# The last feed-forward group in seven products instead of eight, interleaved with the group before it

## The chip, the cores and the metric

The kernel runs on one core of a Trainium2 chip. The metric is device time in microseconds (us) of one execution, the median of several. In the profile, PE is TensorE (matmuls), PEld its weight loads, DVE is VectorE, ACT is ScalarE, POOL is GpSimd and SP is SyncE, which issues most DMAs.

## The reference

Two stages. The first is a retention layer (attention without softmax, with a decay per head) over 8 batches, 8 heads, 576 positions and 64 values per head; the second is a two-layer feed-forward block on the 4608 rows that come out of it.

```
scores = scale * np.matmul(q, k.transpose(0, 1, 3, 2))
Dmat = np.where(rel >= 0, gamma[:, None, None] ** rel[None, :, :], 0.0)
attn = np.matmul(scores * Dmat[None, :, :, :], v)
x = attn.transpose(0, 2, 1, 3).reshape(B * S, H * D)      # 4608 x 512
h = x @ w_in                                              # 512 x 2048
out = (np.maximum(h, 0.0) ** 2) @ w_out                   # 2048 x 512, fp32
```

## The kernel before

**Units and groups.** The 4608 rows are cut into 36 units of 128 rows: four full chunks of a batch, and a "tail" unit that holds the last 64 rows of two batches. Two units make a group, so there are 18 groups, numbered 0 to 17. Per group the retention stage (scores, state sums, outputs; line L337 in the profile) leaves a transposed activation `xT` of 512 x 256. The feed-forward stage (`add_ff`) then makes 16 "FF1 blocks" of four matmuls with 256 columns each (L819). Two blocks share a PSUM bank; ACT takes it out with a relu (L827), and a square follows, on ACT (L837) or on DVE (L839). The squares fill `gT`, the 2048 x 256 input of the second layer. In this text "block 2.1 of group 4" is the second block of the third pair.

**The second layer in seven products.** Groups 0, 1 and 17 multiply `gT` with `w_out` directly, 16 matmuls of 512 columns for each unit (L860; the very last unit by halves of its columns, with a copy and a store for each half). Groups 2 to 16 go through `add_strassen`: the two units, the two halves of the 2048 inner values and the two halves of the 512 output columns make a 2 x 2 x 2 block product, which takes seven products of 8 matmuls with 256 columns instead of eight (L912). Differences of `w_out` (`wT`, L772) are made once. Four sums of the group's `gT` (`gS`, L890) are made by DVE for each group, each in two halves: S3 = A11 - A21, S1 = A21 + A22, S2 = S1 - A11, S4 = A12 - S2. Product P7 reads S3, P6 reads S2, P5 reads S1 and P3 reads S4. Bank "a" gathers P1, P6, P5 and P3 one on top of the other, and after each of the first three ACT copies what stands there (`p1`, `u2`, `u4`, L925). Bank "b" has P2 and bank "c" P7 and then P4. DVE adds banks and copies into the output tile: d11 = b + p1, d22 = c + u4 (this must be done before P4 adds to bank c), d21 = c + u2 (L935); ACT copies the fourth quarter (L955). SP stores each unit with one DMA (L792, L796).

**The order.** No order is written out by hand. Every piece of work is a task with an engine, a key, an assumed duration, its dependencies and the buffers that it takes and frees. `Schedule.emit` plays all of them through, on each engine always the ready task with the lowest key, and the instructions are issued in the order that comes out; after that each engine runs its own list strictly in order. An assumed duration or latency that is changed can therefore move the order of every engine. A DMA's results count as there 2.1 us after its issue slot. Keys of the feed-forward stage count in the units' time, 32 for a unit: FF1 block n of a group has the key `base + 2 n`, the products follow with `base2 + 0, 4, 8 ...`. Forty "warm" matmuls on a scratch tile (L241) have the highest key and fill PE in the front, where weights and inputs arrive (`FIRST` is the order of these loads; the weights are cast by ACT and POOL in halves, L316).

**Around the change.** The units of the last group are reversed, so that its first unit is the tail and its second a full one; its key base is that of the tail unit, after the whole of group 16. Its stores are issued by ACT's queue (L788). From group 11 to 16 the retention of one group is "joined" with the next group's scores; up to group 10 it is not, and then the outputs (`ret/fb`, L337) wait for the state sums, which DVE makes between the sums gS and the addition d22.

Of the kernel before, what the change touches and what calls it, by code (L numbers as in the profile page):

```python
# [9 lines left out]
FP32 = mybir.dt.float32  # L10
FP16 = mybir.dt.float16
ACTF = mybir.ActivationFunctionType
ALU = mybir.AluOpType
# [88 lines left out]
def kernel(  # L102
# [9 lines left out]
    nc = tc.nc  # L112
# [3 lines left out]
    P = 128  # L116
# [31 lines left out]
    g_pool = ctx.enter_context(tc.tile_pool(name="g", bufs=3))  # L148
    u_pool = ctx.enter_context(tc.tile_pool(name="u", bufs=1))
    r_pool = ctx.enter_context(tc.tile_pool(name="r", bufs=3))  # L150
# [64 lines left out]
    for hp in range(NP):  # L215
# [8 lines left out]
    EARLY = 20  # L224
    SQ_ACT = (0, 1, 2, 3, 4, 5, 6)
    JOIN = 11
    PAIRED = 8
    FIRST = ["k0", "q0", "v0", "k2", "q2", "w0", "v2", "w1", "w2", "w3", "w4", "w5", "w6", "w7", "k4", "q4", "v4", "k6", "q6", "v6"]
    sched = Schedule(dict(ff=4, prS=1, prO=1, g=3, ld=5, wst=4, kq=7, v16=7, rT=4, x=3, rl=3, o=4, p1=1, u2=1, u4=1,
                          R=6, Rm=6, kqT=6))  # L230
# [31 lines left out]
    def dma_task(key, dur, fn, **kw):  # L262
        t = add("SP", key, dur, fn, deps=list(last_load), **kw)
        last_load[:] = [t]
        return t
# [18 lines left out]
    def add_load_pair(name, u):  # L284
        b, c = units[u][1:]
        n = "kqv".index(name)

        def fn():
            if name != "q":
                tile_of["stage", u] = stage.tile([P, 2, H, 2 * D], FP32, name="pair", tag="wst")  # L290
            x = tile_of[name + "32", u] = tile_of["stage", u][:, n % 2]
            nc.sync.dma_start(out=x, in_=(k, q, v)[n][b, :, c * P:(c + 2) * P, :].rearrange("h (p e) d -> p h (e d)", e=2))
        loaded[name, u] = loaded[name, u + 1] = dma_task(0, 1.81 if loaded else 2.9, fn, acq=("wst",) if name != "q" else ())

    def add_weight(i):
        fb = i % 4

        def fn():
# [6 lines left out]
            tile_of["w", i] = t  # L305
        t = dma_task(0, 2.75, fn, acq=("wst",))
        dst = w_in16[:, :, fb * 512:(fb + 1) * 512] if i < 4 else w_out16[:, fb * 4:(fb + 1) * 4, :]
# [477 lines left out]

    def store(u, o, lo=0, hi=DM):
        kind, b, c = units[u]

        eng = nc.scalar if group_of[u] == len(groups) - 1 else nc.sync
        if kind == "full":  # L790
            r0 = b * S + c * P
            eng.dma_start(out=out[r0:r0 + P, lo:hi], in_=o[:, lo:hi])  # L792
        else:
            for i in range(2):
                r0 = (b + i) * S + 512
                eng.dma_start(out=out[r0:r0 + 64, lo:hi], in_=o[i * 64:(i + 1) * 64, lo:hi])  # L796
# [8 lines left out]
    def add_ff(g):  # L805
        us = groups[g]
        n = len(us)
        base = us[0] * L
        nf = 4 // n
        f1 = []  # L810
        sq = []
        for fb in range(NF // nf):
            for j in range(nf):
                def f(fb=fb, j=j):
                    if j == 0:
                        tile_of["ph", g, fb] = ps_ff.tile([P, nf, n * P], FP32, name="ph", tag="ff")
                    fi = nf * fb + j
                    for m in range(NP):
                        nc.tensor.matmul(tile_of["ph", g, fb][:, j, :], lhsT=w_in16[:, m, fi * P:(fi + 1) * P],  # L819
                                         rhs=tile_of["x", g][:, m, :], start=(m == 0), stop=(m == NP - 1))  # L820
                f1.append(add("PE", base + (nf * fb + j) * n, 0.01 + 0.2133 * n, f,
                              deps=[T["x", u] for u in us] + wcast_of(nf * fb + j) + f1[-1:],
                              acq=("ff",) if j == 0 else ()))
# [4 lines left out]

            on_act = n == 2 and g >= STRASSEN and fb in SQ_ACT

            def fg(fb=fb, on_act=on_act):
# [6 lines left out]
                else:  # L838
                    nc.vector.tensor_tensor(out=t, in0=rl, in1=rl, op=ALU.mult)  # L839
            r = add("ACT", base + 4 * fb + 4, 0.6, fr, deps=[f1[-1]], acq=("rl",))  # L840
            sched.free("ff", [r])
            sq.append(add("ACT" if on_act else "DVE", base + 4 * fb + 6, 0.63 if on_act else 0.45, fg, deps=[r] + sq[:1],
                          acq=() if fb else ("g",)))
            sched.free("rl", [sq[-1]])
        sched.free("x", [f1[-1]])
        base2 = base + NF * n
        if STRASSEN <= g < len(groups) - 1:
            add_strassen(g, us, base2, sq)
            return
        for s, u in enumerate(us):  # L850
            end = base2 + NF * (s + 1)
            f2 = T["ff2"][-1:] if s == 0 else f2[-1:]

            cuts = [(0, DM)] if u != groups[-1][-1] else [(0, HM), (HM, DM)]
            for ci, (lo, hi) in enumerate(cuts):
                for fi in range(NF):
                    def f(fi=fi, s=s, u=u, lo=lo, hi=hi):
                        if fi == 0:
                            tile_of["po", u, lo] = ps_ff.tile([P, hi - lo], FP32, name="po", tag="ff")
                        nc.tensor.matmul(tile_of["po", u, lo], lhsT=tile_of["g", g][:, fi, s * P:(s + 1) * P],  # L860
                                         rhs=w_out16[:, fi, lo:hi], start=(fi == 0), stop=(fi == NF - 1))
                    f2.append(add("PE", base2 + NF * s + fi / len(cuts) + 8 * ci, 0.0025 + 0.2135 / len(cuts), f,
                                  deps=[sq[fi // nf]] + wcast[4 + fi // 4] + f2[-1:],
                                  acq=("ff",) if fi == 0 else ()))

                def fo(u=u, lo=lo, hi=hi):
                    if lo == 0:
                        tile_of["o", u] = o_pool.tile([P, DM], FP32, name="o", tag="o")
                    nc.scalar.copy(out=tile_of["o", u][:, lo:hi], in_=tile_of["po", u, lo])
                oc = add("ACT", end + 1, 0.12 + 0.47 / len(cuts), fo, deps=[f2[-1]], acq=() if lo else ("o",))  # L870
                sched.free("ff", [oc])
                st = add(*(("ACT", end + 1.1, 0.05) if g == len(groups) - 1 else ("SP", -0.5, 0.7)),
                         lambda u=u, lo=lo, hi=hi: store(u, tile_of["o", u], lo, hi), deps=[oc], after=2.5)
            sched.free("o", [st])
        sched.free("g", [f2[-1]])
        T["ff2"].append(f2[-1])

    def add_strassen(g, us, base, sq):
        uA, uB = us
        G = lambda s, i, h: tile_of["g", g][:, i * HF + h * HF // 2:i * HF + (h + 1) * HF // 2, s * P:(s + 1) * P]  # L880
# [18 lines left out]
        s3[0]["acq"] = ("wst",)  # L899
        s1 = add_sum(0, base, lambda h: G(1, 0, h), lambda h: G(1, 1, h), ALU.add, lambda h: low(h) + high(h) + s3[:1])  # L900
        s2 = add_sum(1, base + 1, lambda h: Sx(0, h), lambda h: G(0, 0, h), ALU.subtract, lambda h: [s1[h]])
        s4 = add_sum(3, base + 4, lambda h: G(0, 1, h), lambda h: Sx(1, h), ALU.subtract, lambda h: [s2[h]])
        last = T["ff2"][-1:]
# [34 lines left out]

        p1 = product(1, 0, "a", raw(0, 0), wB[0, 0], low, True, True, [])
        c1 = on_act_copy("p1", "a", 5, [p1])  # L940
        p7 = product(7, 4, "c", summed(2), wT[2], lambda h: [s3[h]], True, True, [])
        p6 = product(6, 8, "a", summed(1), wT[1], lambda h: [s2[h]], False, True, [c1])
        c2 = on_act_copy("u2", "a", 13, [p6])
        p2 = product(2, 12, "b", raw(0, 1), wB[1, 0], high, True, True, [])
        d11 = on_dve_add(uA, 0, "b", "p1", 17, [p2, c1], ("o",))
        sched.free("ff", [d11])
        sched.free("p1", [d11])
        p5 = product(5, 16, "a", summed(0), wT[0], lambda h: [s1[h]], False, True, [c2])
        c4 = on_act_copy("u4", "a", 21, [p5])
        d22 = on_dve_add(uB, 1, "c", "u4", 22, [p7, c4], ("o",))  # L950
        sched.free("u4", [d22])
        p3 = product(3, 20, "a", summed(3), wB[1, 1], lambda h: [s4[h]], False, True, [c4])

        def f12():
            nc.scalar.copy(out=o_tile(uA)[:, HM:], in_=bank("a"))  # L955
        c12 = add("ACT", base + 25, 0.37, f12, deps=[p3, d11])
        sched.free("ff", [c12])
        p4 = product(4, 24, "c", raw(1, 1), wT[3], high, False, True, [d22])
        d21 = on_dve_add(uB, 0, "c", "u2", 29, [p4, d22])
        sched.free("ff", [d21])  # L960
        sched.free("u2", [d21])
        sched.free("wst", [p3])
        sched.free("g", [p4])
        T["ff2"].append(p4)
        for u, ds in ((uA, [d11, c12]), (uB, [d22, d21])):
            st = add("SP", -0.5, 0.7, lambda u=u: store(u, o_tile(u)), deps=ds, after=2.5)
            sched.free("o", [st])

# [43 lines left out]
```

## Time and profile before

| | |
|---|---|
| median of 4 runs | 298.94 us (298.76 to 299.13) |
| the profiled execution | 299.05 us, of which the span, first to last instruction, is 297.2 |
| PE | busy 286.0 us, 96% of the span, 4320 matmuls |
| DVE, ACT, POOL | busy 199.0, 187.4 and 93.3 us |
| granted TensorE clock | 0.998 of full speed |
| FF1 (L819) | 1152 matmuls |
| seven-product second layer (L912) | 840 matmuls |
| direct second layer (L860) | 112 matmuls |
| squares on ACT (L837) and on DVE (L839) | 112 at 630 ns, 32 at 554 ns |
| sums gS (L890) | 120, at 516 to 591 ns |

A line of the page gives a source line, an engine, an operation, its output and inputs with their shapes, a count, the busy time in us, the mean of one in ns, and the idle time of the engine just before it with what ended that idle time. The busy time of a matmul is longer than its share of PE, since matmuls overlap: what one costs is read from the distance of their starts.

### The profile page before, as it was taken

To read this page: it belongs to the slowest core of one execution; us is meant where nothing else is said; L and a number is where in the kernel's file an instruction comes from. 1 tells how busy PE (TensorE), PEld (TensorE's weight loads), DVE (VectorE), ACT (ScalarE), POOL (GpSimd) and SP (SyncE) were. 2 spreads that over 40 slices of the span, in tenths; PEclk is the share of its full clock that TensorE was granted. 3 is DMA by queue.
4 is the path that set the end of the run, shared out by engine and by line. 5 is a ranking of instruction groups with operands and counts; after the bars stand their busy time and mean duration, and the time that the engine had idled before them with its cause. 6 is when DMAs were issued, how large, how long until landed. Compare 5 with 4: busy or idle time off the path is not lost.

```text
span 297.2 us, 10048 instructions
## 1 busy us (share of the span) xinstructions
PE 286.0 (96%) x4320; PEld 233.4 (79%) x4320; DVE 199.0 (67%) x413; ACT 187.4 (63%) x354; POOL 93.3 (31%) x129
## 2 busy tenths in 40 slices
PE   8979999999989999999999999999999999999995
PEld 3558755688878888888788888788888888988874
DVE  4778469879495949593959597767777766462410
ACT  5247753484867676648576667756666666658861
POOL 4454384434232506152415142424241520000000
PEclk9999999999999999999999999999999999999999
DMA  7999999899999989999969699999999980101012
GB/s 204 326 372 386 360 263 228 213 193 175 210 144 216 195 190 169 209 185 211 178 157 165 151 186 214 213 161 211 156 213 156 218 146 18 73 3 71 2 71 73
DMA packets 139261, 54.14 MB, mean 182 GB/s; under 512 B 118096, under 2 KB 130640, under 8 KB 139216
## 3 DMA queue, kind: packets, MB, share of 16 engines
q1 hardware_dynamic: 138768, 52.97, 85.3%
q8 instruction: 34, 0.56, 0.8%
q10 hardware_dynamic: 448, 0.52, 0.6%
q14 instruction: 11, 0.09, 0.1%
HBM read 36.70 MB, written 9.44 MB: 155 GB/s over the span
## 4 chain that ended last, share of the span: by engine, by line
PE 63%; DVE 12%; ACT 10%; DMA 9%; issue 3%; POOL 2%; POOLq 0%
PE po L912 26%; PE ph L819 25%; DVE gS L890 6%; ACT rl L827 5%; ACT gT L837 4%; PE psO L337 4%; PE po L860 4%; DMA pair<-in_v_dram 3%; DMA wo<-in_moe_w_out_dram 3%; DMA pair<-in_k_dram 3%; PE warm L241 2%; DVE gT L839 2%; PE psc L337 1%; PE psS L337 1%; PE psT L412 1%
## 5 line engine op out<-in xcount | busy, mean ns | idle before, releaser
L819 PE MATMUL ph<-xT,w_in 128*128 128x256 f16 x1152 | 139.4, 273 | 0.0
L819 PEld LDWEIGHTS <-w_in 128*128 128x128 f16 x1152 | 111.2, 98 | 14.9 <-POOL w_in L316 0.3
L827 ACT ACTIVATE rl<-ph 128x512 f16<-128x512 f32 x144 | 84.1, 588 | 51.7 <-PE ph L819 49.1
L837 ACT ACTIVATE gT<-rl 128x512 f16<-128x512 f16 x112 | 70.6, 630 | 3.5
L890 DVE TENSOR_TENSOR gS<-gT 128x512 f16<-128x512 f16 x60 | 33.6, 560 | 39.1 <-ACT gT L837 38.5
L912 PEld LDWEIGHTS <-gS 128*128 128x128 f16 x480 | 45.6, 98 | 10.0 <-DVE gS L890 4.5
L912 PE MATMUL po<-wT,gS 128*128 128x256 f16 x360 | 49.2, 273 | 2.4 <-DVE gS L890 2.3
L361 POOL TENSOR_TENSOR v<-v,vdec_full 128x512 f16<-128x512 f32 x24 | 25.7, 1072 | 57.2 <-DMA v<-in_v_dram 48.2
L912 PEld LDWEIGHTS <-gT 128*128 128x128 f16 x360 | 34.8, 98 | 4.4 <-issue 0.2
L912 PE MATMUL po<-w_out,gT 128*128 128x256 f16 x240 | 31.1, 273 | 0.0
L349 POOL CAST kq<-k 128x512 f16<-128x512 f32 x28 | 18.8, 672 | 35.1 <-DMA k<-in_k_dram 34.7
L349 POOL CAST kq<-q 128x512 f16<-128x512 f32 x28 | 18.4, 656 | 27.1 <-DMA q<-in_q_dram 27.0
L839 DVE TENSOR_TENSOR gT<-rl 128x512 f16<-128x512 f16 x32 | 17.6, 554 | 13.6 <-ACT rl L827 13.2
L860 PE MATMUL po<-w_out,gT 128*128 128x512 f16 (+1 forms) x112 | 22.6, 349 | 0.1
L925 ACT COPY u<-po 128x256 f32<-128x256 f32 x30 | 11.0, 367 | 15.7 <-PE po L912 15.4
L698 DVE TENSOR_TENSOR xT<-psO,gam_full 128x512 f16<-128x512 f32 x28 | 18.4, 685 | 2.9 <-PE psO L337 2.6
L935 DVE TENSOR_TENSOR o<-po,u 128x256 f32<-128x256 f32 x30 | 12.6, 418 | 10.5 <-PE po L912 7.2
L637 DVE TENSOR_TENSOR rT<-psc,mask 128x512 f16<-128x512 f32 x28 | 18.5, 680 | 1.1 <-PE psc L337 1.1
L890 DVE TENSOR_TENSOR gS<-gS,gT 128x512 f16<-128x512 f16 x30 | 17.7, 591 | 1.0
L860 PEld LDWEIGHTS <-gT 128*128 128x128 f16 x112 | 10.6, 98 | 7.9 <-issue 0.3
L890 DVE TENSOR_TENSOR gS<-gT,gS 128x512 f16<-128x512 f16 x30 | 15.4, 516 | 1.0
L912 PE MATMUL po<-wT,gT 128*128 128x256 f16 x120 | 15.8, 273 | 0.2 <-DVE o L935 0.2
(78 smaller groups left out, 263.5 us busy)
## 6 DMA issues: line engine op xcount, KB each, us to landing
out_dram<-o SPq DMA_DIRECT2D x31, 256.0 KB, 2.7
k<-in_k_dram SPq DMA_DIRECT2D x24, 256.0 KB, 4.7
q<-in_q_dram SPq DMA_DIRECT2D x24, 256.0 KB, 5.2
v<-in_v_dram SPq DMA_DIRECT2D x24, 256.0 KB, 4.7
wi<-in_moe_w_in_dram SPq DMA_DIRECT2D x4, 1024.0 KB, 10.1
wo<-in_moe_w_out_dram SPq DMA_DIRECT2D x4, 1024.0 KB, 9.4
pair<-in_k_dram SPq DMA_DIRECT2D x4, 512.0 KB, 5.8
pair<-in_q_dram SPq DMA_DIRECT2D x4, 512.0 KB, 5.7
```

The costliest lines, as they stand in the source:

```text
L337: nc.tensor.matmul(out_, lhsT=lhsT, rhs=rhs, start=start, stop=True, skip_group_check=True, tile_position=(64 * row, 64 * col))
L349: op(out=out_.rearrange("p (n b a d) -> p n b a d", n=2, b=2, a=2), in_=in_.rearrange("p (n a b) d -> p n b a d", n=2, a=2))
L361: nc.gpsimd.tensor_tensor(out=t, in0=tile_of["v32", u], in1=vdec[kind].rearrange("p (h o) -> p h o", o=1).to_broadcast([P, H, D]), op=ALU. ...
L637: nc.vector.tensor_tensor(out=r, in0=tile_of["psc", g][:, :, cols(s)].rearrange("p a (n i) -> p a n i", i=64), in1=mask.rearrange("p (o r ...
L698: nc.vector.tensor_tensor(out=tile_of["x", g][:, :, s * P:(s + 1) * P].rearrange("p n (c i) -> p c n i", c=2), in0=tile_of["psO", g][:, :, ...
L819: nc.tensor.matmul(tile_of["ph", g, fb][:, j, :], lhsT=w_in16[:, m, fi * P:(fi + 1) * P], rhs=tile_of["x", g][:, m, :], start=(m == 0), st ...
L827: nc.scalar.activation(out=t, in_=tile_of["ph", g, fb], func=ACTF.Relu)
L837: nc.scalar.activation(out=t, in_=rl, func=ACTF.Square)
L839: nc.vector.tensor_tensor(out=t, in0=rl, in1=rl, op=ALU.mult)
L860: nc.tensor.matmul(tile_of["po", u, lo], lhsT=tile_of["g", g][:, fi, s * P:(s + 1) * P], rhs=w_out16[:, fi, lo:hi], start=(fi == 0), stop= ...
L890: nc.vector.tensor_tensor(out=Sx(k, h), in0=in0(h), in1=in1(h), op=op)
L912: nc.tensor.matmul(tile_of["pb", g, bank], lhsT=left(i), rhs=right[:, i, :], start=(start and i == 0), stop=(i == HF - 1), skip_group_chec ...
```

## The change

Seven things are changed together.

1. The last group, 17, also goes through `add_strassen`. Its FF1 blocks get keys (`place`, `SPREAD`) that put them right behind those of group 16, ahead of group 16's second layer. Of its seven products P1, P6, P5 and P3 (the quarter in bank "a", which needs nothing else) get keys between those of group 16; P2, P7 and P4 come at the end.
2. P4 of the last group has a bank of its own ("e") and is made by halves of its columns, 16 matmuls with 128 columns. Bank c + u2 is put aside by DVE before that (`f7`), and the last addition is made in two halves (`fd`).
3. The last group's stores are cut: four quarters of a unit, the last of them in two halves of 128 columns. d11's and d22's are issued by ACT, the others by SP.
4. In all groups S2 is made as A22 - S3 instead of S1 - A11, so it doesn't need S1; its key is lower, S1's is higher by one.
5. The last two groups make the squares of three pairs of blocks (1, 4, 6) on ACT instead of seven.
6. The planner counts the results of loads v2, w1, k4 and q4 as there 1.2, 1.3, 0.7 and 0.5 us later than the other loads.
7. The buffers p1, u2 and u4 are there twice.

```diff
-    u_pool = ctx.enter_context(tc.tile_pool(name="u", bufs=1))
+    u_pool = ctx.enter_context(tc.tile_pool(name="u", bufs=2))
...
+    SPREAD = 0.1
+    SQ_LATE = (1, 4, 6)
+    LAG = {"v2": 1.2, "w1": 1.3, "k4": 0.7, "q4": 0.5}
...
-        t = dma_task(0, 2.75, fn, acq=("wst",))
+        t = dma_task(0, 2.75, fn, acq=("wst",), after=2.1 + LAG.get(f"w{i}", 0.0))
...
-        base = us[0] * L
+        base = min(us) * L
+
+        def place(x):
+
+            return base + x if g < last_g else base - NF * n - 1 + SPREAD * x
...
-            on_act = n == 2 and g >= STRASSEN and fb in SQ_ACT
+            on_act = g >= STRASSEN and fb in (SQ_ACT if g < last_g - 1 else SQ_LATE)
...
-        if STRASSEN <= g < len(groups) - 1:
+        if STRASSEN <= g:
             add_strassen(g, us, base2, sq)
...
-        s1 = add_sum(0, base, lambda h: G(1, 0, h), lambda h: G(1, 1, h), ALU.add, lambda h: low(h) + high(h) + s3[:1])
-        s2 = add_sum(1, base + 1, lambda h: Sx(0, h), lambda h: G(0, 0, h), ALU.subtract, lambda h: [s1[h]])
-        s4 = add_sum(3, base + 4, lambda h: G(0, 1, h), lambda h: Sx(1, h), ALU.subtract, lambda h: [s2[h]])
+        early = 12 if g == last_g else 0
+        s2 = add_sum(1, base - 4 - early, lambda h: G(1, 1, h), lambda h: Sx(2, h), ALU.subtract, lambda h: high(h) + [s3[h]])
+        s1 = add_sum(0, base + 1 - early, lambda h: G(1, 0, h), lambda h: G(1, 1, h), ALU.add, lambda h: low(h) + high(h) + s3[:1])
+        s4 = add_sum(3, base + 4 - early, lambda h: G(0, 1, h), lambda h: Sx(1, h), ALU.subtract, lambda h: [s2[h]])
...
+        if g == last_g:
+            last[:] = []
+            at = -2 * NF * n
+            p1 = product(1, at + 3.5, "a", raw(0, 0), wB[0, 0], low, True, True, [])
+            c1 = on_act_copy("p1", "a", at + 8, [p1])
+            p6 = product(6, at + 11.5, "a", summed(1), wT[1], lambda h: [s2[h]], False, True, [c1])
+            c2 = on_act_copy("u2", "a", at + 16, [p6])
+            p5 = product(5, at + 19.5, "a", summed(0), wT[0], lambda h: [s1[h]], False, True, [c2])
+            c4 = on_act_copy("u4", "a", at + 24, [p5])
+            p3 = product(3, at + 27.5, "a", summed(3), wB[1, 1], lambda h: [s4[h]], False, True, [c4])
+            c12 = add("ACT", base + 1, 0.37, f12, deps=[p3], acq=("o",))
+            p2 = product(2, 12, "b", raw(0, 1), wB[1, 0], high, True, True, T["ff2"][-1:])
+            d11 = on_dve_add(uA, 0, "b", "p1", 17, [p2, c1, c12])
+            p7 = product(7, 16, "c", summed(2), wT[2], lambda h: [s3[h]], True, True, [])
+            def f7():
+                t = tile_of["p1", g] = u_pool.tile([P, HM], FP32, name="p1", tag="p1")
+                nc.vector.tensor_tensor(out=t, in0=bank("c"), in1=tile_of["u2", g], op=ALU.add)
...
+                        for i in (2 * q, 2 * q + 1):
+                            nc.tensor.matmul(bank("e")[:, sl], lhsT=raw(1, 1)(i), rhs=wT[3][:, i, sl],
+                                             start=(x == 0 and i == 0), stop=(i == HF - 1), skip_group_check=True)
...
+            d22 = on_dve_add(uB, 1, "c", "u4", 21, [p7, c4], ("o",))
+            d7 = add("DVE", base + 22, 0.42, f7, deps=[d22, c2], acq=("p1",))
...
+                    nc.vector.tensor_tensor(out=o_tile(uB)[:, sl], in0=bank("e")[:, sl], in1=tile_of["p1", g][:, sl],
+                                            op=ALU.add)
+                d21.append(add("DVE", base + 29 + x, 0.25, fd, deps=[p4s[x], d7]))
...
+                for d, lo, hi in ((d11, 0, HM), (c12, HM, DM)) if u == uA else ((d22, HM, DM), (d21[0], 0, HM // 2),
+                                                                                (d21[1], HM // 2, HM)):
+                    eng = ("ACT", base + 25.1, 0.05) if d is d11 or d is d22 else ("SP", -0.5, 0.05)
```

The branch for the other groups keeps its products, copies and additions as they were. The branch of `add_ff` for groups 0 and 1 loses the cut by halves, which only the last unit used.

## The prediction

> **What bounds the kernel now.** I read the page first, then a table of stretches, then the waits, then the order of time around the longest waits and at both ends.
>
> ```profile
> span 297.2 us, 10048 instructions
> PE 286.0 (96%) x4320; PEld 233.4 (79%) x4320; DVE 199.0 (67%) x413; ACT 187.4 (63%) x354; POOL 93.3 (31%) x129
> ...
> PE 63%; DVE 12%; ACT 10%; DMA 9%; issue 3%; POOL 2%; POOLq 0%
> ```
>
> TensorE is busy 96% of the span, so what counts is its own work, and each place where it stands. The stretches (length, then busy time of PE, PEld, DVE, ACT, POOL) show where: three of five middle ones have 0.6 to 0.8 us without PE, and the last one, after the last matmul, 3.1 us.
>
> ```profile
> 79.00:94.00 15.00, 14.23 (x244) 12.10 (x243) 12.13 (x22) 9.67 (x19) 5.07 (x7) 1.00 1.00 180
> 94.00:109.00 15.00, 14.83 (x242) 12.66 (x240) 11.15 (x22) 9.77 (x20) 5.34 (x7) 1.00 1.01 195
> 109.00:124.00 15.00, 14.41 (x246) 12.56 (x244) 11.60 (x22) 9.34 (x19) 4.81 (x6) 1.00 0.94 185
> 124.00:139.00 15.00, 14.90 (x237) 12.85 (x236) 9.96 (x19) 9.78 (x20) 5.90 (x7) 1.00 1.07 201
> 139.00:154.00 15.00, 14.33 (x237) 12.23 (x235) 11.65 (x22) 9.78 (x19) 4.67 (x6) 1.00 0.90 165
> ...
> 287.00:297.20 10.20, 7.09 (x50) 4.59 (x47) 0.43 (x1) 2.90 (x6) 0.00 (x0) 0.95 0.19 53
> ```
>
> The waits name what PE stands for in the middle: the sums of L890, made by DVE.
>
> ```profile
> PEld L912 <- DVE gS L890: 4.5, 8, 1.0
> ...
> PE po L912 <- DVE gS L890: 2.3, 5, 0.7
> ```
>
> Start to start I find the matmul before the second half of P6 late by 0.84 us in group 3, 0.26 in 4, 0.73 in 7, 0.13 in 8, 0.68 in 10, 0.12 in 11, 0.43 in 12 and 0.44 in 13: 3.6 us in all. DVE in order of time in group 3 shows why, and what comes after (start, duration):
>
> ```profile
> 80.88 0.41 DVE L839 TENSOR_TENSOR gT<-rl 128x512 f16<-128x512 f16 x1
> 81.33 1.22 DVE L890 TENSOR_TENSOR gS<-gT 128x512 f16<-128x512 f16 x1
> 82.58 0.80 DVE L890 TENSOR_TENSOR gS<-gS,gT 128x512 f16<-128x512 f16 x1
> ...
> 87.32 0.91 DVE L666 TENSOR_TENSOR R<-stmp,dec 128x256 f16<-128x256 f32 x1
> 88.16 0.41 DVE L935 TENSOR_TENSOR o<-po,u 128x256 f32<-128x256 f32 x1
> ```
>
> The last square, then S1, then S2, and only then P6 (83.44). DVE goes on without a gap to the addition at 88.16 (d22), which P4 (88.83) needs. The front, and PE's clean pace, then the end:
>
> ```profile
> 19.76 0.44 PE L337 MATMUL psS<-vx,kx 64*64 64x64 f16 x32 [1.67 <-POOL vx L393]
> 21.02 1.24 PE L241 MATMUL warm<-junk 128*128 128x512 f16 x5
> 22.10 1.48 PE L819 MATMUL ph<-xT,w_in 128*128 128x256 f16 x12
> ...
> 12.04 0.61 PE L412 MATMUL psT<-ident,kx 128*128 128x128 f16 x8
> 12.49 0.81 PE L241 MATMUL warm<-junk 128*128 128x512 f16 x3
> ...
> 294.13 0.37 ACT L869 COPY o<-po 128x256 f32<-128x256 f32 x1 [1.19 <-PE po L860]
> 294.53 0.34 ACTq L792 DMA_DIRECT2D out_dram<-o  x1
> ```
>
> A 256-column matmul is repeated every 0.109 us, so one FF1 block (4 of them) is 0.437 us and one product (8) is 0.874 us. Eight with 128 columns take 12.49 - 12.04 = 0.45 us, 0.056 each.
>
> **The sum** is made against the profiled execution, 299.05 us (span 297.2 and 1.85 around it); the median of the runs is 298.94, 0.11 lower.
>
> **1. The last group in seven products (gain 0.80 on PE).** Removed: 16 matmuls of 512 columns and 32 of 256, 286.98 to 293.93, 6.95 us. Added: six products of 8 matmuls, 48 x 0.109 = 5.24, and P4 as 16 matmuls of 128 columns, 16 x 0.056 = 0.90; 6.14. PE is never waiting in 274 to 287 (13.00 of 13.00 busy), so 0.80 comes off the end if the new order does not wait. I walked it with the rows' durations. All 16 FF1 blocks of group 17 now follow those of group 16, 28 blocks on end, 0.873 us for each pair of blocks; a relu costs ACT 0.6 and three squares in eight 0.63 each, (8 x 0.6 + 3 x 0.63) / 8 = 0.84 a pair, under 0.873. The eight squares that move from ACT to DVE, four in each of the last two groups (0.43 each there), lie where DVE is busy 4.25 of 13 us. Group 17's P1, P6, P5, P3 alternate with group 16's products, so each copy out of bank a (0.2 after the matmul, then 0.37) has 0.87 us or more of other products over it. Its sums are made before P6 of group 16 ends. Nothing waits, up to P7. Without that cover each copy would show with 0.57. If the weight loads of P4 (98 ns each on PEld) did not overlap, it would take 16 x 0.098 = 1.57 and leave a gain of 0.13.
>
> The Trainium skill ("TensorE: Matmul & The Clock Gate", Back-to-back issue gap) gives about 81 ns for a sustained 128-column matmul with its weight load, which speaks against P4 in halves: 16 x 0.081 = 1.30, and the gain would be 0.40. The L412 rows here, weight load before each matmul too, show 0.056; I go by them.
>
> **2. Behind the last matmul (gain 0, to 0.2).** Before: 0.20 to the copy, 0.37, issue at 294.53, the semaphore of SP at 296.28 (1.75 on), 0.94 to the end. After: P7 ends at 292.23 by the same sum; DVE then runs d22 (0.42), f7 (0.42) and the two halves of the last addition one behind the other. A 256-column addition is 0.42 and a 512-column one 0.69, so 128 columns take 0.42 - 0.13 = 0.29. That ends at 293.7. SP has to issue the first half (0.35) before the second, which therefore goes out at 293.95, 0.58 before the 294.53 of now: of the 0.80 0.22 is lost to DVE and SP. The last store is 64 KB instead of 128 KB; the packets of the present one take 0.53 us (295.37 to 295.90), so half saves 0 to 0.26; I take 0.12. Steps 1 and 2 together: **-0.70**, between -0.95 (all of the smaller store) and 0 (loads that do not overlap, or one uncovered copy).
>
> **3. S2 from S3, in groups 2 to 16.** S2 no longer stands behind S1: after the last square, P6 waits for one sum instead of two. In group 3 that takes 0.84 off the wait. But the order is made by a planner, which now brings P6 forward: one FF1 block fewer stands between P7 and the second half of P6 in groups 3, 4, 5, 7, 8, 9, 12, 13 and 15, two fewer in 10, one more in 2, 6 and 14. That 0.44 of cover is gone, and comes later. Against the time at which S2 would be ready (last square plus the duration of the sum in that place) the wait at P6 becomes 0.1, 0.3, 0, 0.1, 1.0, 0, 0.1 and 0.1 for groups 3, 4, 8, 7, 10, 11, 12, 13: 1.7 instead of 3.6, a gain of 1.9. What is late next is DVE. S1, S2 and S4 are all still made, so d22 comes no sooner, and P4 of the unjoined groups stands within 0.05 to 0.3 us of it (88.57 against 88.83 in group 3, 119.39 against 119.45 in group 5). In groups 3, 5 and 7 the new order puts FF1 block 2.1 of the next group behind P4 instead of ahead of it: 0.44 that used to lie under DVE's chain is then paid after it, and its relu and square delay the next group's by 0.3. Walking P4 from group to group with these rows: group 3 -0.1, 5 and 6 together +0.4, 7 (which had its block behind P4 already) -0.1 and 8 +0.1, 9 0, 10 +0.2, 11 -0.1, 12 -0.4, 13 -0.3, 14 and 15 0. Sum **-0.30**. The ends: all waits for sums gone, -3.6; no wait gone and 0.44 lost in each of the six groups 3, 4, 5, 7, 8, 9, +2.6.
>
> **4. The front (0).** With the later load times the planner puts FF1 blocks 1.0 and 1.1 of group 0 ahead of the sums that wait for v (19.76). That fills 0.87 of the 1.67, but block 2.0 needs the cast of the second w_in tile, which ends at 22.03 as before: it still starts at 22.10, with five warm matmuls before it. ACT now casts w_in tiles 2 and 3 ahead of the relus of blocks 2 and 3, which queue behind a DMA; four PSUM banks carry that. Three FF1 blocks of group 1 that filled PE while w_in 3 and w_out 0 arrived (casts until 27.64 and 30.03) now come later: 3 x 0.44 = 1.3 lost. They fill the waits of 0.28 (37.67), 0.42 (40.54), 0.23 (42.76) and 0.35 (48.56), 1.28. Net 0, between -0.35 (the last of the four filled and nothing lost) and +0.7 (the first two not filled). On SP two stores and a transpose change places with loads of units 9 to 14, at 0.35 an issue; POOL's order does not change. Nearest row: POOL waits 52.5 us for v in all, none of it PE's; 0.
>
> **Sum:** 299.05 - 0.70 - 0.30 + 0 = 298.05, less 0.11 to a median: **298.0 us**.
>
> **Rivals.**
> A, slower: DVE's chain takes over. Place: P4 behind d22 in the unjoined groups. For it: the gapless chain above and the 0.05 of group 5. Against: group 4 has 0.6 us of room, 8 has 0.3. If each of the four groups 4, 5, 8 and 9 loses the block (4 x 0.44 = 1.75): 299.0 + 1.75 - 0.7 = 300.1. It decides when the middle costs over 1.3 us, three blocks.
> B, much faster: the wait at P6 was what set the pace and d22 is early enough, so 1.9 is kept: 298.9 - 1.9 - 0.7 = 296.3. For it: the chain of waits runs through the sums in groups 3, 4, 5, 7, 10, 12, 13. Against: DVE has no gap behind them.
> C, no change: the end does not gain (a stand in the 28 blocks, where PSUM banks and ACT have little room, or weight loads that show), the middle as forecast, front +0.2: 298.9 - 0.3 + 0.2 = 298.8.
>
> **Chances.** Forecast 0.45, its own range 297.2 to 298.7; B 0.22; C 0.18; A 0.15. 0.2% is 0.6 us, about what a measurement of this kernel can tell from no change: faster is below 298.34, slower above 299.54. Faster: 0.37 of the forecast, 0.22 of B and 0.03 of C, 0.62. Slower: 0.13 of A and 0.02 of C, 0.15. The rest, 0.23, within. The range 296.2 to 299.9 leaves out the low part of B and the top of A.
>
> **What will show it.** Step 1: PE without a gap from P1 of group 16 to the end, and the last matmul about 0.8 us nearer to the start of group 16's FF1. Step 2: L-lines of the halved addition one behind the other on DVE, the last issue some 1.7 us before SP's semaphore. Step 3: PE's late starts behind gS down from 3.6 us to about half, and a new wait of PE for the additions o (or P4 directly behind one). Step 4: FF1 of group 2 starting at 55.5 as now. I am wrong if the waits for sums vanish without new ones, or if the middle stretches lose PE time.

## The result and the profile after

The changed kernel takes 297.68 us (median of 41 runs, 295.56 to 299.18) against 298.81 for the kernel before (65 runs, 297.46 to 300.38). The ratio is 0.9958, 95% interval 0.9947 to 0.9969: faster by 0.4%. Forecast were 298.0 us, a range of 296.2 to 299.9, and faster as the likeliest sign.

The time fits the forecast's total; its terms do not fit. The profiled execution took 298.74 us, span 296.9. First the page of the changed kernel: its span, the PE line and the shares of the chain.

```profile
span 296.9 us, 10096 instructions
PE 285.2 (96%) x4336; PEld 235.4 (79%) x4336; DVE 203.5 (69%) x434; ACT 183.2 (62%) x347; POOL 95.2 (32%) x129
...
PE 74%; DVE 11%; ACT 6%; DMA 5%; issue 2%; POOL 1%; SPq 0%; DVEq 0%
```

PE's share of the chain rises from 63% to 74%, at the expense of ACT (10 to 6%) and DMA (9 to 5%); DVE's hardly falls (12 to 11%). Now the waits of PE and then of its weight loads, in the changed kernel (total us, times, longest).

```profile
PE psO L341 <- DVE stmp L666: 1.4, 2, 0.9
...
PE ph L825 <- POOL w_in L320: 1.2, 2, 0.8
PE po L914 <- DVE o L937: 0.9, 3, 0.6
...
PE po L914 <- DVE gS L891: 0.5, 1, 0.5
...
PEld L914 <- DVE gS L891: 1.5, 4, 0.8
```

The waits for the sums gS fell from 2.3 and 4.5 us to 0.5 and 1.5. Two others have grown in this execution: the outputs of the retention (`psO`) wait for the state sums `stmp` (0.3 before), and the products for the addition `o` (0.2 before). New in front, blocks of FF1 wait for `w_in`. So in this execution the middle stretches (length, then busy time of PE, PEld, DVE, ACT, POOL) are no fuller than before; the last one shows the shorter work at the end.

```profile
79.00:94.00 15.00, 13.97 (x242) 12.10 (x241) 11.89 (x22) 8.60 (x18) 5.83 (x7) 1.00 0.92 178
...
109.00:124.00 15.00, 14.42 (x246) 12.56 (x245) 11.03 (x22) 9.10 (x19) 4.91 (x6) 1.00 0.91 176
...
139.00:154.00 15.00, 14.27 (x237) 12.44 (x235) 11.48 (x22) 8.93 (x19) 4.89 (x6) 1.00 0.91 167
...
287.00:297.20 10.20, 6.32 (x66) 5.58 (x64) 2.52 (x7) 1.49 (x4) 0.00 (x0) 0.94 0.34 104
```

Group 3 shows the longest of these waits. The changed kernel in order of time there, rows of DVE, POOL and PE (start, duration):

```profile
81.07 1.15 DVE L891 TENSOR_TENSOR gS<-gT,gS 128x512 f16<-128x512 f16 x1
82.14 0.82 DVE L891 TENSOR_TENSOR gS<-gT 128x512 f16<-128x512 f16 x1
82.89 0.82 DVE L891 TENSOR_TENSOR gS<-gT,gS 128x512 f16<-128x512 f16 x1
...
85.35 1.24 DVE L670 TENSOR_TENSOR R<-stmp,dec 128x256 f16<-128x256 f32 x1
...
87.56 0.42 DVE L666 TENSOR_TENSOR stmp<-psS,Rm 128x256 f32<-128x256 f32 x1
...
88.36 0.42 DVE L937 TENSOR_TENSOR o<-po,u 128x256 f32<-128x256 f32 x1
...
85.27 1.04 POOL L365 TENSOR_TENSOR v<-v,vdec_full 128x512 f16<-128x512 f32 x1 [1.83 <-DMA v<-in_v_dram]
...
88.04 0.19 PE L341 MATMUL psO<-kqT,Rm 64*64 64x64 f16 x1 [0.93 <-DVE stmp L666]
...
88.96 1.05 PE L914 MATMUL po<-wT,gT 128*128 128x256 f16 x8
89.84 0.38 PE L825 MATMUL ph<-xT,w_in 128*128 128x256 f16 x2
```

S2 (81.07) is made right after the last square, before S1 (82.14). Then DVE's chain goes on as before, and `stmp` ends at 87.98. PE came to the retention outputs 0.93 us too early, and FF1 block 2.1 (89.84) stands behind P4 (88.96), where it fills nothing. An instruction of DVE that takes 0.42 us elsewhere took 1.24 beside POOL's multiplication at 85.27; more on that below.

At the end of the changed kernel, in order of time:

```profile
292.26 1.06 PE L976 MATMUL po<-wT,gT 128*128 128x128 f16 x16
292.52 0.42 DVE L937 TENSOR_TENSOR o<-po,u 128x256 f32<-128x256 f32 x1 [0.50 <-PE po L914]
292.86 0.41 DVE L966 TENSOR_TENSOR p<-po,u 128x256 f32<-128x256 f32 x1
...
293.38 0.49 DVE L988 TENSOR_TENSOR o<-po,p 128x128 f32<-128x128 f32 x2
293.70 0.81 SPq L794 DMA_DIRECT2D out_dram<-o  x2
```

The last matmul starts at 293.10 (293.82 before), the last store is issued at 294.13 (294.53 before), the span ends at 296.93 (297.22 before). Of the 0.72 us that PE is earlier, 0.29 arrives at the end.

### The profile page after: what moved, and what is told of

It is laid out like the page before. It is cut to its first block, busy times and chain, and to the rows that moved or that the text cites. A ratio compares the mean times of both kernels' runs of the same rounds, so it can differ in the third digit from the quotient of the medians.

```text
span 296.9 us, 10096 instructions
## 1 busy us (share of the span) xinstructions
PE 285.2 (96%) x4336; PEld 235.4 (79%) x4336; DVE 203.5 (69%) x434; ACT 183.2 (62%) x347; POOL 95.2 (32%) x129
## 4 chain that ended last, share of the span: by engine, by line
PE 74%; DVE 11%; ACT 6%; DMA 5%; issue 2%; POOL 1%; SPq 0%; DVEq 0%
PE ph L825 33%; PE po L914 27%; PE po L863 5%; DVE gS L891 4%; PE psO L341 4%; DMA wo<-in_moe_w_out_dram 3%; ACT rl L833 3%; ACT gT L843 3%; DMA pair<-in_q_dram 2%; PE psc L341 2%; PE warm L244 1%; PE psS L341 1%; DVE rT L641 1%; PE psT L416 1%; DVE R L670 1%
## 5 line engine op out<-in xcount | busy, mean ns | idle before, releaser
L843 ACT ACTIVATE gT<-rl 128x512 f16<-128x512 f16 x104 | 65.6, 631 | 3.0
L914 PEld LDWEIGHTS <-gS 128*128 128x128 f16 x512 | 49.3, 98 | 7.3 <-DVE gS L891 1.5
L914 PE MATMUL po<-wT,gS 128*128 128x256 f16 x384 | 52.2, 273 | 0.5 <-DVE gS L891 0.5
L891 DVE TENSOR_TENSOR gS<-gT,gS 128x512 f16<-128x512 f16 x64 | 37.2, 582 | 21.5 <-ACT gT L843 20.9
L914 PEld LDWEIGHTS <-gT 128*128 128x128 f16 x376 | 36.5, 98 | 5.3 <-issue 0.8
L914 PE MATMUL po<-w_out,gT 128*128 128x256 f16 x256 | 34.5, 273 | 0.0
L845 DVE TENSOR_TENSOR gT<-rl 128x512 f16<-128x512 f16 x40 | 19.2, 483 | 14.6 <-ACT rl L833 13.9
L914 PE MATMUL po<-w_out,gS 128*128 128x256 f16 x128 | 16.6, 273 | 0.0
L863 PE MATMUL po<-w_out,gT 128*128 128x512 f16 x64 | 15.6, 379 | 0.2 <-POOL w_out L320 0.2
L670 DVE TENSOR_TENSOR R<-stmp,dec 128x256 f16<-128x256 f32 x24 | 14.4, 600 | 0.7
```

Of the source, the lines that this page charges most:

```text
L843: nc.scalar.activation(out=t, in_=rl, func=ACTF.Square)
L863: nc.tensor.matmul(tile_of["po", u], lhsT=tile_of["g", g][:, fi, s * P:(s + 1) * P], rhs=w_out16[:, fi, :], start=(fi == 0), stop=(fi == N ...
L891: nc.vector.tensor_tensor(out=Sx(k, h), in0=in0(h), in1=in1(h), op=op)
L914: nc.tensor.matmul(tile_of["pb", g, bank], lhsT=left(i), rhs=right[:, i, :], start=(start and i == 0), stop=(i == HF - 1), skip_group_chec ...
```

## The experiments

The first four runs took the change apart, beside the changed kernel once more and all against the kernel before on one chip.

**The changed kernel again.** No edit.

> The changed kernel once more, on the chip of the next three. The first profile of it shows the end 0.4 us earlier at the last store's issue and the front and middle level with before (+0.04 us at P1 of group 15), while the medians differ by 1.1 us. Theory: the middle differs from execution to execution, with the moments at which POOL's casts fall on DVE's sums, and another profile shows it up to 1 us earlier. Rival: the profiled execution is typical, and the gain lies behind the span; then this profile too has the middle within 0.1 us of before.

Measured: 297.65 us (12 runs), ratio 0.9980 (0.9960 to 1.0000). The gain is less sure in size than the first comparison said: 0.2% here, 0.4% there. Its profiled execution took 296.31 us, 2.4 less than the first one of the very same program, and the whole difference is in the middle. One stretch, 56 to 256, of the first and of the second execution:

```profile
56.00:256.00 200.00, 196.32 (x3253) 170.19 (x3252) 144.53 (x291) 131.93 (x253) 65.62 (x81) 1.00 0.96 177
```

```profile
56.00:256.00 200.00, 198.12 (x3276) 172.04 (x3275) 140.20 (x292) 134.39 (x257) 66.05 (x81) 1.00 0.96 180
```

For about the same instructions DVE is busy 4.3 us less, and PE stands 1.8 us less. The 0.93 us in group 3 are gone in the second execution, though PE's order is the same. The list of PE's waits there has none for `stmp`; those for the sums and for `o`, and then rows of group 3, are:

```profile
PE po L914 <- DVE gS L891: 0.6, 1, 0.6
PE po L914 <- DVE o L937: 0.5, 1, 0.5
...
84.97 0.41 DVE L670 TENSOR_TENSOR R<-stmp,dec 128x256 f16<-128x256 f32 x1
86.35 0.42 DVE L666 TENSOR_TENSOR stmp<-psS,Rm 128x256 f32<-128x256 f32 x1
...
87.81 1.04 POOL L365 TENSOR_TENSOR v<-v,vdec_full 128x512 f16<-128x512 f32 x1 [3.19 <-DMA v<-in_v_dram]
```

POOL's multiplication comes 2.5 us later there, `R<-stmp,dec` takes 0.41 instead of 1.24, and `stmp` ends at 86.77 instead of 87.98. A single profile of this kernel is therefore good to about 2 us in the middle, and parts are compared by medians and by the order of instructions.

**The end alone** (new last group, its squares, stores and doubled buffers; S2 of the other groups and load times as before; the edit is against the changed kernel):

```diff
-    LAG = {"v2": 1.2, "w1": 1.3, "k4": 0.7, "q4": 0.5}
+    LAG = {}
...
...
+        else:
+            s1 = add_sum(0, base, lambda h: G(1, 0, h), lambda h: G(1, 1, h), ALU.add, lambda h: low(h) + high(h) + s3[:1])
+            s2 = add_sum(1, base + 1, lambda h: Sx(0, h), lambda h: G(0, 0, h), ALU.subtract, lambda h: [s1[h]])
```

> The change without S2 from S3 in groups 2 to 16 and without the later load times: only the last group in seven products, its place, its squares and its stores. Forecast by step 1 and 2: 0.7 us faster than before, ratio 0.9977; by the first profile's end 0.3 to 0.4 us, ratio 0.9988. If the end gains nothing (rival C): 1.000.

Measured: 297.34 us, ratio 0.9985 (0.9961 to 1.0009). About 0.45 us, and not certainly different from nothing. From FF1 of group 2 to group 15 PE's order is the one of the kernel before, task by task, and the sums are made as before. Yet in this profile PE waits for them less than half as long as the 2.3 us of the profile before:

```profile
PE po L918 <- DVE gS L891: 1.1, 3, 0.5
```

The 3.6 us of late starts that step 3 sets out from are therefore those of one execution too.

**S2 from S3 alone** (edit against the kernel before):

```diff
-        s1 = add_sum(0, base, ...)
-        s2 = add_sum(1, base + 1, lambda h: Sx(0, h), lambda h: G(0, 0, h), ALU.subtract, lambda h: [s1[h]])
+        s2 = add_sum(1, base - 4, lambda h: G(1, 1, h), lambda h: Sx(2, h), ALU.subtract, lambda h: high(h) + [s3[h]])
+        s1 = add_sum(0, base + 1, ...)
```

> Before with S2 = A22 - S3 and its keys alone. Step 3: the waits of P6 fall from 3.6 us to about 1, new waits of PE for the state sums and d22 of DVE take most of it, net -0.3 us, ratio 0.999. Rival B: 1.9 us faster, ratio 0.9936. Rival A: up to 1.75 us slower, ratio 1.006.

Measured: 296.13 us, ratio 0.9935 (0.9909 to 0.9961). A gain of 1.9 us, the size that rival B gave it. In its profile PE has no wait of 0.2 us or more for the sums gS, and one of 0.3 for `o`. This one of three parts alone is faster than the whole, by 1.5 us on the same chip.

**The later load times alone** (edit against the kernel before: `LAG` and the two `after=2.1 + LAG.get(...)`):

> Before with the later load times of the planner alone (v2, w1, k4, q4). Step 4: no difference, ratio 1.000, group 2's FF1 starts within 0.3 us of before. If the three FF1 blocks of group 1 are not made up for: up to 0.7 us slower, ratio 1.002. If the wait of 1.67 us is really gained: 0.994.

Measured: 298.56 us, ratio 1.0019 (1.0002 to 1.0035): a loss of about 0.5 us (0.06 to 1.04) where I had said 0.

So the parts do not add up: -0.45, -1.9 and +0.5 make -1.85 together, and the whole gains 0.6 to 1.25. The next four runs, on another chip, set out from the changed kernel without the later load times.

**The changed kernel without the later load times** (`LAG = {}`):

> The changed kernel without the later load times. Its order keeps block 2.1 of the next group ahead of P4 in groups 3, 5 and 7, where the changed kernel has it behind P4. Theory: the later load times cost their 0.5 us of the run before, and 0.44 us more in each of the three groups; without them S2 from S3 and the end add up, ratio 0.992 to before (0.9935 and 0.9985). Rival: the later load times only cost the 0.0019 that they cost alone, ratio 0.995 to 0.996.

Measured: 296.17 us, ratio 0.9934 (0.9909 to 0.9958). Without them the changed kernel is 1.5 us faster by the medians, 0.7 to 1.4 by the ratios; the interval holds the theory's 0.992 and part of the rival's 0.995 to 0.996. The size is more than their loss alone and points to the middle. PE's order in group 3 shows it (F = FF1 block of group 4, fa and fb = retention, fb the outputs):

```
before                     P1 P7 fa F0.0 F0.1 P6 F1.0 P6 P2 P5 F1.1 F2.0 P3 F2.1 fb P4 F3.0
changed                    P1 P7 fa F0.0 P6 F0.1 P6 P2 F1.0 P5 F1.1 F2.0 P3 fb P4 F2.1 F3.0
changed, no later loads    P1 P7 fa F0.0 F0.1 P6 P2 F1.0 P5 F1.1 F2.0 P3 F2.1 fb P4 F3.0
```

From FF1 of group 2 to group 15 this last order is the same, task by task, as with S2 from S3 alone. Block 2.1 stands behind P4 in groups 2, 4, 6, 8, 11, 13, 14 and 15 there, with the later load times in 3, 5, 7, 10 and 12 to 15. The number is the same. But in the profile before, P4 starts only 0.26, 0.05 and 0.25 us behind the end of DVE's d22 in groups 3, 5 and 7, and 0.60, 0.33, 0.88 and 0.63 behind it in 4, 8, 11 and 13. (Groups 10 and 12 have 0.89 and 0.18.) That this room makes the same number of lost blocks dearer is argued, not shown. The later load times change in the planner which groups lose the block.

**S2 counted later by the planner.** A loss that remains is that the planner, which now sees S2 early, takes one FF1 block away from ahead of the second half of P6. In this version, otherwise the one without later load times, it counts S2's result 0.45 us late:

```diff
-                out_.append(add("DVE", key + h, 0.45, f, deps=deps(h)))
+                out_.append(add("DVE", key + h, 0.45, f, deps=deps(h), after=0.57 if k == 1 and g < last_g else None))
```

> As the kernel without the later load times, but the planner counts S2 as there 0.45 us later (in groups 2 to 16), so that PE's FF1 blocks stand ahead of P6 as they did before; DVE still makes S2 ahead of S1. Theory that the lost cover ahead of P6 costs: 0.3 to 1 us faster than the kernel without the later load times. Theory that DVE's chain up to d22 sets P4 and the cover doesn't matter: within 0.2 us of it.

Measured: 295.15 us, ratio 0.9907 (0.9876 to 0.9939), 1 us faster than without the late count; the two intervals overlap, and the version is run once more below. PE's order from FF1 of group 2 to group 15 is now, task by task, the one of the kernel before. In the stretch 56 to 256 PE is busy 199.1 of 200 us; the row of the kernel before stands first:

```profile
56.00:256.00 200.00, 196.36 (x3251) 169.00 (x3250) 148.91 (x291) 131.83 (x253) 63.64 (x80) 1.00 0.98 177
...
56.00:256.00 200.00, 199.09 (x3287) 173.27 (x3285) 139.94 (x293) 134.99 (x260) 65.32 (x82) 1.00 0.97 180
```

**One sum fewer on DVE.** The version without later load times; S4 is not made, and P3 reads S2 in its place:

```diff
+                    if k != 3:
                         nc.vector.tensor_tensor(out=Sx(k, h), in0=in0(h), in1=in1(h), op=op)
...
-            p3 = product(3, 20, "a", summed(3), ...)
+            p3 = product(3, 20, "a", summed(1), ...)
```

> As the kernel without the later load times, but S4 is not made, and P3 reads S2 in its place: two sums of 0.42 to 0.75 us fewer on DVE in each of groups 2 to 17, in the same order. If DVE's chain (sums, state sums, d22) holds PE in the unjoined groups, the waits ahead of ret/fb and P4 go: 1 to 2.5 us faster. If PE alone is the bound: within 0.3 us.

Measured: 295.69 us, ratio 0.9922 (0.9895 to 0.9949). Two sums fewer in each of 16 groups (DVE is busy 182.2 us instead of 197.1) buy 0.5 us, and the intervals overlap. PE's order from FF1 of group 2 to group 15 is the same in both. DVE's chain may cost the middle something, but it does not set its pace: that would have bought 1 us or more.

**POOL casts k twice.** The version without later load times, the cast of k made twice from unit 8 on:

```diff
-            sorted_cast(nc.gpsimd.tensor_copy, t[:, 0], tile_of["k32", u])
+            for again in range(2):
+                sorted_cast(nc.gpsimd.tensor_copy, t[:, 0], tile_of["k32", u])
```

> As the kernel without the later load times, but POOL casts k of each unit from 8 on twice (28 more casts of 0.65 us; POOL is busy 31% of the span, and PE never waits for these casts). If casts that fall on DVE's sums make these long (0.42 alone, up to 1.3 beside POOL), and the spread of the middle is made by that: 0.5 to 2 us slower. If not: within 0.2 us.

Measured: 297.09 us, ratio 0.9976 (0.9943 to 1.0008), 0.9 us slower by the medians, and the runs spread from 295.39 to 299.67. The groups of POOL of this kernel (count, busy us, mean ns):

```profile
L353 POOL CAST kq<-k 128x512 f16<-128x512 f32 x56 | 37.9, 678 | 32.0 <-DMA k<-in_k_dram 28.7 <-PE ph L826 1.0
```

28 casts more, some 18 us of an engine that is busy a third of the time. Part of the 0.9 us may be the later casts themselves, part DVE's longer sums beside POOL (DVE is busy 203.0 us here and 197.1 in the version it is compared with); this run does not separate the two.

The last four runs stand on one chip (before: 298.70 us).

**The best version once more.**

> The best version so far once more (no later load times, S2 counted 0.45 us late, new end), on the chip of the three runs above, so that they can be compared with it. 295.0 to 295.5, ratio to before 0.988 to 0.993. If it comes at 296 or above, the planner's late count of S2 bought nothing and the first run was a draw of the spread between executions.

Measured: 295.39 us, ratio 0.9893 (0.9857 to 0.9930). Confirmed: this version beats both kernels, the one before by 2.8 to 3.3 us in its two runs.

**The later load times, with S2 counted late.** The best version with `LAG` as in the changed kernel.

> The changed kernel with its later load times, S2 counted 0.45 us late. In this order FF1 block 2.1 of the next group stands ahead of the retention outputs and of P4 in groups 3, 5, 7 and 8, as in the version without later load times; the front keeps the order that the later load times make. Theory 'the later load times cost by what they do to the middle's order': the time is within 0.3 us of the version without them (about 295.2 to 295.5, ratio to before 0.990 to 0.992), and no wait before ret/fb or P4 above 0.3 us. Rival 'they cost in the front': about 0.6 us slower than that version (ratio 0.993), and FF1 of group 2 starts later by as much.

Measured: 295.53 us, ratio 0.9904 (0.9873 to 0.9935), 0.14 from the best version, within the noise. With the late count, which gives the middle another order, the later load times cost little, so most of their price in the changed kernel lies in that order. PE in group 3 of this kernel (start, duration):

```profile
85.83 1.04 PE L825 MATMUL ph<-xT,w_in 128*128 128x256 f16 x8
86.71 1.04 PE L914 MATMUL po<-w_out,gS 128*128 128x256 f16 x8
87.67 0.21 PE L341 MATMUL psO<-kqT,Rm 64*64 64x64 f16 x1
...
88.60 1.05 PE L914 MATMUL po<-wT,gT 128*128 128x256 f16 x8
89.48 0.71 PE L825 MATMUL ph<-xT,w_in 128*128 128x256 f16 x5
```

Blocks 2.0 and 2.1 (85.83) are ahead of P3 (86.71), and the outputs follow without a wait. (The second execution of the changed kernel has none there either, so this place alone does not show the price.) This is the order of the middle of the run with the later load times alone, task by task. In the front something is left: FF1 of group 2 starts at 55.66 to 55.83 in the four profiles with later load times and at 55.34 to 55.64 in the ten without, 0.27 later in the mean. The wait is for the cast of `w_in`, here as in the changed kernel:

```profile
PE ph L825 <- POOL w_in L320: 1.2, 2, 0.8
```

**The best version with the old end** (the kernel before, S2 from S3, S2 counted late; every engine's order is the one of the kernel before, but for S1 and S2, which change places on DVE in 15 groups):

> Before, with S2 = A22 - S3 and S2 counted 0.45 us late; the last group in eight quarters as before, no later load times. Theory 'end and middle add up': slower than the version with the new end by the end's 0.45 us (0.3 to 0.8), so 295.6 to 296.0, ratio to before 0.992 to 0.9935. Rival 'the end buys nothing': level with it, 295.2. In the profile: waits of PE for sums under 0.3 us in all in groups 2 to 16, last matmul end to the last store issue 0.6 us as before.

Measured: 295.51 us, ratio 0.9900 (0.9867 to 0.9933), 0.12 from the best version, less than the 0.3 I set as the least. The medians can't tell 0.1 from 0.4; the traces tell more. From the start of P1 of group 15 to the end of the span it takes 37.46 to 37.47 us in the four profiles with the old end, and 37.08 to 37.40, in the mean 37.21, in the nine with the new end in halves. The end is worth 0.25 us, with a spread of 0.3 from one execution to the next. The spread lies wholly behind the last issue: from P1 to it the nine agree to 0.01 us, and from it to the end they take 2.75 to 3.07.

**P4 whole instead of by halves**, in the best version:

```diff
-            for x in range(2):
+            for x in range(1):
...
-                        sl = slice(x * HM // 2, (x + 1) * HM // 2)
+                        sl = slice(0, HM)
...
-                for d, lo, hi in (...) if u == uA else ((d22, HM, DM), (d21[0], 0, HM // 2), (d21[1], HM // 2, HM)):
+                for d, lo, hi in (...) if u == uA else ((d22, HM, DM), (d21[0], 0, HM)):
```

> The best version so far (no later load times, S2 counted 0.45 us late), with P4 of the last group whole: 8 matmuls of 256 columns, one addition of 256 columns after it, one store of 128 KB from SP. In the profile of the changed kernel the last matmul ends at 293.21 and f7 only at 293.27 (292.86 + 0.42), the halved additions follow at 293.38 and 293.58, SP issues at 293.70 and 294.13. Theory 'halves save little, since DVE (d22, f7) and SP's issues stand one behind the other anyway': whole, the addition starts at 293.3 and ends at 293.7, one issue at 293.85 to 294.2 instead of the second at 294.13; the store is longer by 0 to 0.26 us. The time is within 0.25 us of the halved version (ratio between the two 0.999 to 1.001). Rival 'the halving carries the end's gain': 0.58 us slower or more, since the whole 0.42 addition and the 128 KB store come behind P4.

Measured: 295.35 us, ratio 0.9898 (0.9865 to 0.9931), 0.04 from the halves. Its end in order of time:

```profile
289.15 1.04 PE L976 MATMUL po<-wT,gT 128*128 128x256 f16 x8
...
289.75 0.41 DVE L966 TENSOR_TENSOR p<-po,u 128x256 f32<-128x256 f32 x1
290.27 0.42 DVE L988 TENSOR_TENSOR o<-po,p 128x256 f32<-128x256 f32 x1
...
290.72 0.34 SPq L794 DMA_DIRECT2D out_dram<-o  x1
```

Start of P4 to the one issue: 1.57 us; in the changed kernel, start of P4 (292.26) to the second issue (294.13): 1.87. To the end of the span it is 4.69 here and 4.67 there: the whole store takes longer by what its issue is earlier. From P1 of group 15 to the end it is 37.16, among the 37.08 to 37.40 of the halves. The halving buys nothing that these runs can tell.

## Why the prediction was right in its total and wrong in its terms

**Step 1 was right** (gain 0.80 on PE). P1 of group 15 to the last matmul's start takes 34.06 us before and 33.30 to 33.31 in the nine profiles with this end, 0.75 less. P4's 16 matmuls of 128 columns start from 292.26 to 293.10, 0.056 apart. Against the 81 ns of the Trainium skill ("TensorE: Matmul & The Clock Gate", Back-to-back issue gap) the row of the kernel before was the better guide.

**Step 2 was mis-sized.** I lost 0.22 to DVE and SP and won 0.12 with the smaller store. In the changed kernel, last matmul start to last issue grew from 0.71 to 1.03 (0.32 lost): the first issue of SP is at 293.70, where the forecast's times give 293.60, and the second comes 0.43 behind the first and not 0.35. From this issue to the end of SP's wait for the store's semaphore it is 1.75 in both: the smaller store wins nothing, where I had 0.12. (In the nine profiles with halves it is 1.70 to 2.01, with the whole store 2.06.) And there is a term that I did not have: SP ends the kernel with a list of waits, and behind the one for the last store now stand four more rows instead of two, at 0.06 each: 1.05 us to the end instead of 0.94. The term "-0.70 for steps 1 and 2" is -0.33 in this pair of profiles (37.46 to 37.13 us from P1 of group 15 to the end) and -0.25 over all of them.

**Step 3 failed, in size and in cause.** "Net -0.30" was the term. Alone, S2 from S3 gains 1.9 us; with all of PE's order kept as before it gains 3.0 (ratio 0.9900, the run with the old end), near the bound "all waits for sums gone, -3.6". The place of the working that failed is the loss set against it, "in groups 3, 5 and 7 the new order puts FF1 block 2.1 behind P4". I read this from the order of the whole change and put it down to S2's new key. It takes both: the new S2 alone puts the block behind P4 in groups 2, 4, 6, 8, 11 and 13 to 15, the later load times alone in 6, 13 and 15 (before: 2, 6, 14 and 15), and only the two together in 3, 5 and 7. The working also names 3, 5 and 7 alone, though the changed order has the block behind P4 in 10, 12 and 13 too, and calls the one of group 7 behind P4 already, which in the kernel before is ahead of it. That DVE's chain is what comes next was half right at most. The waits for `stmp` and `o` are 2.3 us in the first execution and 0.5 in the second, and 15 us less work on DVE moved the time by 0.5 only, less than the 1.0 that the place of the fillers is worth, though the intervals of the two overlap.

**Step 4 failed.** "Net 0" for the later load times looked at the front alone. There it was off by 0.27, inside its bounds of -0.35 to +0.7. Their greater price is in the middle: they change the planner's order up to group 15. With S2 from S3 the whole of it is 0.7 to 1.5 us; with the late count, by which the block is behind P4 in groups 6, 13 and 15 only and P6 keeps most of its cover, 0.14. Which of the two places in the order costs how much, the runs do not separate.

**The rivals.** B was right in its mechanism, the wait at P6 did set the pace; the later load times kept its gain from showing. What A counted on, a new order that loses blocks as cover, is there: it takes 1 us without the later load times (296.17 against 295.15) and some 2 with them (ratios 0.9958 and 0.9980 against 0.9904), but against a gain of 3 and not of 1.9. That DVE's chain takes over, as A had it, is not what the run without S4 shows. C's doubt of the end was in part right: it gains a third of the 0.70. The total came right by luck, because the errors stood against each other: alone, S2 from S3 gains 1.6 us more than my net 0.30, the end gains 0.45 less than my 0.70, and the later load times take 0.9 to 1.55 where I had 0 (what is left of 1.9 and 0.25 to the measured 0.6 to 1.25; taking them out gave 0.7 to 1.5). The likeliest case's own range of 297.2 to 298.7 held the time; its story did not hold.

Left open: why the last stores take up to 0.3 us longer in some executions (in the three longest ends the first half lands 2.13 to 2.23 us after its issue, in the other six 1.70 to 1.95), and how much of the 0.9 us of doubled casts is due to DVE's longer sums.

## What to carry to other kernels

Where a planner orders the work, a faster operation is also an earlier one in the planner's eyes, and may lose the fillers that stood ahead of it: compare the order of instructions part by part, and try the new operation with the old order before it is judged. A part that "only touches the front" has to be followed through the whole order, and a loss seen in the order of the whole change may belong to two parts together: look at the order of each part alone before you put it down to one. A wait seen in one profile should be looked for in a second one of the same program. Work that was cut at the end arrives only as far as the engines, issues and semaphore waits behind the last matmul let it.

## What the runs showed of the hardware

The two profiled executions of the changed kernel differ by 2.4 us, all of it in the middle, at a granted clock of 1.00 in the middle stretch of both. In every profile the sums gS, the squares on DVE and `R<-stmp,dec`, which have two inputs in SBUF, the memory of the tiles, take 0.42 to 0.43 us when no POOL instruction runs beside them, and are mostly longer when one does. In the changed kernel's first profile 74 sums gS without POOL beside them have a mean of 0.420 and a longest of 0.43; 40 that overlap a POOL instruction by over 0.3 us have a mean of 0.83 and a longest of 1.28. Instructions with an input in PSUM, the memory of the banks, are not lengthened: `stmp<-psS,Rm` is 0.42 in 13 cases without and in 7 cases with POOL beside it, `rT<-psc,mask` 0.68 in both, the additions `o` 0.42 in both.

The Trainium skill says this ("SBUF — State Buffer", Who interferes with whom): a DVE instruction with two SBUF inputs contends with a GpSimd instruction that reads SBUF, and one with at most one, outside the modes that use both ports, doesn't. The trace agrees. In group 3 of the changed kernel this is most of what separates the two executions: `R<-stmp,dec` took 1.24 us beside POOL and 0.41 without, 0.83 of the 1.21 us by which `stmp` ended later. That it makes the whole spread between executions is argued, not shown: for the same 434 instructions DVE is busy 203.5 us in the first execution and 198.3 in the second.
